# Sinks of two attention forms: their products with V one sub-step later at a chunk's end, and in the second attention in one transpose and one burst for all heads

## The chip, the cores and the metric

The kernel runs on one core of a Trainium2 chip. The metric is the device time of one execution, in microseconds (us). The engines' names in the profile are PE (TensorE, with PEld for its weight loads), DVE (VectorE), ACT (ScalarE), POOL (GpSimd) and SP (SyncE, which issues most DMAs).

## What is computed

Attention with a window of 128 and 4 sink positions, over 4 batches, 8 heads, 768 positions and 64 columns a head; its result, seen as 3072 tokens of 512 columns, goes through a gated product with three weight matrices.

```python
keep = is_sink | in_window              # pos < 4, or 0 <= q - k < 128
scores = np.where(keep, scale * q @ k.T, -1e9)
a = np.exp(scores - scores.max(-1, keepdims=True))
a = a / (a.sum(-1, keepdims=True) + 1e-9)
x = (a @ v).transpose(0, 2, 1, 3).reshape(3072, 512)
out = (x @ w_a) * (x @ w_b) @ w_out     # w_a, w_b: 512 x 1536, w_out: 1536 x 512
```

The reference's inputs give each block of 128 queries (a *tile*) three parts of keys: its own block, the block before it, and the 4 sinks.

## The kernel before

**Stages.** The first tiles of the four batches are done ahead (`first_tiles`). Then come chunks: batch 0's tiles 1 and 2 (the *second attention*, exact float32, `first_attention` with `parts_exact` and `pipeline`), four chunks of three tiles of one batch, and two chunks of three tiles from two batches (two *segments*); these six go through `attention` with `parts_split`, where each float32 operand is a high and a low part. While chunk c's gated product (`moe`) runs on TensorE, the attention of chunk c+1 is woven in: `moe` calls `between(s)` at 33 places, and that takes the attention's generator forward by some of its sub-steps (a `yield` each), 21 of the second attention's and 30 of the others'. What is left then is taken after `moe`. A scheduler sets the final order of each engine's instructions, except where they are kept in program order. It follows priorities by program order and moves an instruction where it thinks that its inputs are late.

**The gated product.** For each of 12 blocks of columns, `moe` makes a (12 products of 128 columns of weights, L846: four blocks kk of x, three high/low combinations each), copies it to g on ScalarE (L883), makes b (L846), multiplies on VectorE (L889), splits the result into gh on ScalarE (L892) and gl (L894) on GpSimd, in the chunk of the first tiles on VectorE, and projects the block before (L873, named o_0, o_1, ... by tile). At a chunk's end the outputs are copied (L904) and written (L905); x of the next chunk is split by ScalarE's cast xh (L829) and VectorE's subtraction xl (L830), block by block. x lies in four parts xf[0] to xf[3], one for each pair of heads.

**Sinks, attention().** The scores (L628) give p for the window and for 4 sinks; a predicated copy (L633) and a reduction (L634) read them from the one PSUM buffer "s". The sinks' columns of all 8 heads lie in one tile sc for each query tile. `sinks_t` turns them with three transposes (L668), and ScalarE, VectorE and ScalarE split them (L670 to L672). `sinks_av(m)` multiplies those of pair m with V of the sinks (L679), and VectorE adds the product to xf[m] (L681). Pairs 0 and 2 take PSUM bank "t", 1 and 3 bank "av"; `av` of a pair (L659) uses "av" too and is copied to xf by ScalarE (L661). V of the sinks comes in two groups (pairs 0, 1 and pairs 2, 3), loaded by `prep_sinks` (L435) and split by GpSimd in `split_sinks` (round, L387, and rest, L390). With two segments both groups lie in one region, since each group then holds one part for each segment.

**Sinks, second attention.** p of a pair of heads gives a sc of 8 columns. `sinks_t(pr)` turns it (L777, 8 rows of 128 columns), VectorE copies it into ptx (L779), and `sinks_av(pr)` multiplies it with the pair's V of the sinks (L784, K of 8) and adds to xf (L786). Transposes (L757), `av` (L769) and sinks share one PSUM bank "t" in two halves; one tile stands for the whole bank.

## Time and profile before

| | |
|---|---|
| Median of 3 runs | 757.16 us (756.3 to 757.17) |
| Profiled execution | 756.8 us, span 755.1 us |
| TensorE busy | 745.2 us, 99 % of the span |
| VectorE, ScalarE, GpSimd busy | 389.8, 387.4, 275.5 us |
| Granted TensorE clock | 0.999 of full speed |

The span is the stretch that the profiler sees; the execution's time includes a little around it. A row of a timeline gives an instruction's start, its length, engine, line, operation and tiles; matmuls are pipelined, so the record of one (0.40 us for 512 columns) is longer than the distance to the next start, and it is distances of starts that add up. A bracket names idle time of the engine ahead and what ended it.

### The profile page before, as it was taken

Reading aid. Unit: us, or ns where it says so; the run is one execution under the profiler, and the core shown is the slowest. Engines: PE = TensorE matmul, PEld = TensorE weight load, DVE = VectorE, ACT = ScalarE, POOL = GpSimd, SP = SyncE. Lnnn points to the kernel's source line nnn. Section 1 sums busy time; section 2 is a strip of 40 time slices with the busy share of each in tenths; the row PEclk is TensorE's granted clock in tenths of the full one; section 3 lists DMA queues with packets and bytes.
Section 4 is the critical chain, followed back from the end, with each engine's and each line's share of the span. In section 5 each row is a group of like instructions: output and inputs, shape, how many; then the busy total and the mean of one; then the engine's idle time right before and its main releaser. Section 6 shows DMA issues by size and latency. Waiting matters only on the chain.

```text
span 755.1 us, 13078 instructions
## 1 busy us (share of the span) xinstructions
PE 745.2 (99%) x4422; PEld 665.7 (88%) x4422; DVE 389.8 (52%) x1303; ACT 387.4 (51%) x1185; POOL 275.5 (36%) x358
## 2 busy tenths in 40 slices
PE   8999999999999999999999999999999999999996
PEld 6877777889899998999989999899989999999996
DVE  6899998455455553445544554355553555331001
ACT  6777765466455663555535555355554655331111
POOL 2200021176425542355404545056561764201110
PEclk9999999999999999999999999999999999999999
DMA  9997111322213343124422344124443141010001
GB/s 333 394 318 279 33 40 40 118 72 75 64 46 85 105 141 92 57 85 123 132 82 70 96 126 138 63 75 124 115 121 114 47 132 47 2 42 1 1 1 44
DMA packets 48807, 76.89 MB, mean 102 GB/s; under 512 B 5056, under 2 KB 28640, under 8 KB 48736
## 3 DMA queue, kind: packets, MB, share of 16 engines
q1 hardware_dynamic: 45568, 70.50, 29.6%
q10 hardware_dynamic: 3168, 5.51, 1.9%
q8 instruction: 36, 0.59, 0.3%
q14 instruction: 35, 0.29, 0.1%
HBM read 69.70 MB, written 6.29 MB: 101 GB/s over the span
## 4 chain that ended last, share of the span: by engine, by line
PE 90%; DMA 3%; DVE 3%; ACT 1%; POOL 1%; issue 1%; SPq 0%; DVEq 0%; POOLq 0%; ACTq 0%
PE a L846 26%; PE o L873 25%; PE b L846 25%; PE s L628 5%; PE av L659 5%; PE t L648 2%; DMA raw_a<-in_wa_dram 1%; DMA raw_o<-in_wo_dram 1%; DMA v<-in_v_dram 1%; PE sk L679 1%; PE s L732 1%; DMA qr<-in_qT_dram 1%; PE t L757 0%; PE t L769 0%; DVE wf_o L348 0%
## 5 line engine op out<-in xcount | busy, mean ns | idle before, releaser
L846 PE MATMUL a<-xh,w_a 128*128 128x384 f32 (+2 forms) x760 | 212.3, 342 | 0.1
L846 PE MATMUL b<-xh,w_b 128*128 128x384 f32 (+2 forms) x760 | 209.9, 340 | 0.5 <-DVE w_b L366 0.5
L873 PE MATMUL o<-w_o,gh 128*128 128x512 f32 x576 | 182.4, 398 | 0.0
L894 POOL TENSOR_TENSOR gl<-g,gh 128x384 fp32r<-128x384 f32 (+1 forms) x70 | 68.2, 974 | 225.9 <-ACT gh L892 221.6
L846 PEld LDWEIGHTS a<-xh,w_a 128*128 128x128 f32 x760 | 137.2, 188 | 8.3 <-issue 1.7
L846 PEld LDWEIGHTS b<-xh,w_b 128*128 128x128 f32 x760 | 137.2, 188 | 5.8 <-issue 1.0
L846 PE MATMUL a<-xl,w_a 128*128 128x384 f32 (+2 forms) x380 | 127.8, 336 | 0.0
L846 PE MATMUL b<-xl,w_b 128*128 128x384 f32 (+2 forms) x380 | 127.7, 336 | 0.0
L873 PEld LDWEIGHTS o<-w_o,gh 128*128 128x128 f32 x576 | 103.9, 188 | 18.8 <-issue 0.9
L873 PE MATMUL o<-w_o,gl 128*128 128x512 f32 x288 | 113.3, 394 | 0.0
L889 DVE TENSOR_TENSOR g<-b,g 128x384 f32<-128x384 f32 (+2 forms) x95 | 52.8, 555 | 112.6 <-PE b L846 111.5
L636 ACT ACTIVATE p<-p,st 128x132 f32<-128x132 f32 x144 | 58.0, 403 | 74.4 <-DVE st L634 73.2
L892 ACT CAST gh<-g 128x384 fp32r<-128x384 f32 (+2 forms) x96 | 49.3, 513 | 88.6 <-DVE g L889 88.6
L883 ACT COPY g<-a 128x384 f32<-128x384 f32 (+2 forms) x95 | 45.0, 474 | 91.2 <-PE a L846 85.7
L633 DVE COPY_PREDICATED s<-own,s 128x128 f32<-128x128 uint16 x144 | 42.0, 291 | 82.0 <-PE s L628 80.4
L846 PEld LDWEIGHTS a<-xl,w_a 128*128 128x128 f32 x380 | 71.4, 188 | 2.7
L639 ACT ACTIVATE p<-p,st 128x132 f32<-128x132 f32 x144 | 58.2, 404 | 29.3 <-DVE st L638 28.6
L846 PEld LDWEIGHTS b<-xl,w_b 128*128 128x128 f32 x380 | 71.4, 188 | 1.7
L390 POOL TENSOR_TENSOR ks<-kr,ks 64x524 fp32r<-64x524 f32 (+1 forms) x64 | 70.4, 1110 | 3.9
L873 PEld LDWEIGHTS o<-w_o,gl 128*128 128x128 f32 x288 | 54.1, 188 | 12.9 <-DVE gl L894 0.9
L637 DVE TENSOR_SCALAR st<-st 128x1 f32<-128x1 f32 x144 | 21.9, 152 | 74.8 <-ACT p L636 74.8
L387 POOL TENSOR_SCALAR qh<-qr 128x384 fp32r<-128x384 f32 x48 | 24.9, 519 | 86.4 <-DMA qr<-in_qT_dram 49.4
(166 smaller groups left out, 1029.7 us busy)
## 6 DMA issues: line engine op xcount, KB each, us to landing
raw_a<-in_wa_dram SPq DMA_DIRECT2D x12, 512.0 KB, 7.8
raw_b<-in_wb_dram SPq DMA_DIRECT2D x12, 512.0 KB, 6.3
raw_o<-in_wo_dram SPq DMA_DIRECT2D x12, 512.0 KB, 6.9
qr<-in_qT_dram SPq DMA_DIRECT2D x32, 192.0 KB, 2.6
chk_a<-in_wa_dram SPq DMA_DIRECT2D x24, 256.0 KB, 3.2
chk_b<-in_wb_dram SPq DMA_DIRECT2D x24, 256.0 KB, 3.0
chk_o<-in_wo_dram SPq DMA_DIRECT2D x24, 256.0 KB, 3.1
out_dram<-os ACTq DMA_DIRECT2D x21, 256.0 KB, 2.1
```

The costliest lines, as they stand in the source:

```text
L390: self.nc.gpsimd.tensor_tensor(o, i, high.bitcast(F32), op=ALU.subtract)
L628: nc.tensor.matmul(ps, lhsT=q[:, i * P:(i + 1) * P], rhs=ks[:, c0s[i]:c0s[i] + SW], start=n == 0, stop=n == 1)
L633: nc.vector.copy_predicated(ps[:, :P], self.own.bitcast(mybir.dt.uint16), ps[:, W:])
L636: nc.scalar.activation(p, p, AF.Exp, bias=st[:, 0:1], scale=-1.0, accum_out=st[:, 1:2])
L639: nc.scalar.mul(p, p, st[:, 3:4])
L659: nc.tensor.matmul(ps[half[e], c * P:(c + ns) * P], lhsT=v[:, e, blk, :], rhs=pt[:, e, sl:sl + ns, :], start=j == 0, stop=j == len(groups) ...
L846: mm = self.nc.tensor.matmul(ps[:, cols], lhsT=w[:, ksl], rhs=x[:, kk, cols], start=start and kk == 0 and i == 0, stop=kk == NK - 1 and i ...
L873: nc.tensor.matmul(outs[i], lhsT=g[:, sl], rhs=w, start=j == 0 and k == 0, stop=j == NJ - 1 and k == 2)
L883: nc.scalar.copy(g[:, :n], pa[:, :n])
L889: nc.vector.tensor_tensor(g[:, :n], pb[:, :n], g[:, :n], op=ALU.mult)
L892: nc.scalar.copy(gh[:, :n], g[:, :n])
L894: e.tensor_tensor(gl[:, :n], g[:, :n], gh[:, :n].bitcast(F32), op=ALU.subtract)
```

## The change

In `attention`, `sinks_av(0)`, `sinks_av(1)` and `split(1)` move from the last sub-step of h = 8 to the first one of h = 9; `sinks_av(2)` and `(3)` stay in the second and third. In `parts_exact` and `pipeline` the sinks of all heads are collected in one tile of 32 columns and turned by one transpose, the turned sinks lie in a buffer of the tag "p" (sks) instead of in ptx, the loads of V of the sinks are two instead of four, with all 32 rows and zeros for the other heads' rows (the array vS holds them so), and the four products with K of 32 follow in two sub-steps at the end. The parameter `group` goes. Lines behind the change have lower numbers after it (L846 is L840 after, L873 is L867, L679 is L677).

```diff
--- before.py
+++ after.py
@@ -558,7 +558,7 @@
         (_, t0, nt), = segs
         late = [i for i in range(nt) if t0 + i >= 2]
         units = [(h, i) for h in range(H) for i in range(nt)]
-        return self.pipeline(units, nt, late, *self.parts_exact(*segs[0], xf, after), 2, 2, 1)
+        return self.pipeline(units, nt, late, *self.parts_exact(*segs[0], xf, after), 2, 1)
 
     def attention(self, parts, xf, after):
 
@@ -583,15 +583,13 @@
                         split(0)
                 if i == 1 and 1 <= h <= H:
                     transposes(h - 1)
-                if h == H:
-                    if i == 1:
-                        sinks_t()
-                    elif i == 2:
-                        sinks_av(0, xf)
+                if h == H and i == 1:
+                    sinks_t()
+                elif h > H:
+                    sinks_av(i + (i > 0), xf)
+                    if i == 0:
                         sinks_av(1, xf)
                         split(1)
-                elif h > H and i:
-                    sinks_av(i + 1, xf)
                 yield
 
     def parts_split(self, segs):
@@ -714,11 +712,11 @@
                 nc.sync.dma_start(v[:, :, :nb], self.vB[b, h // 2, :, :, s0:s0 + nb])
             else:
                 v = preps[h - 1][2]
-                if late:
-                    vs = ptx[:2 * NS, h // 2 % 2, 2 * nt + 1, :]
-                    m = h // 2
-                    nc.sync.dma_start(vs, self.vS[b, m * 2 * NS:(m + 1) * 2 * NS, m])
-                    vss[h // 2] = vs
+                if late and h < 4:
+                    vs = ptx[:H * NS, h // 2, 2 * nt:2 * nt + 2, :]
+                    nc.sync.dma_start(vs, self.vS[b, :H * NS, h - 1:h + 1])
+                    for c in range(2):
+                        vss[h - 1 + c] = vs[:, c, :]
             preps[h] = k, q, v
 
         def scores(h, i):
@@ -742,9 +740,9 @@
             nc.scalar.mul(p[:, :w], p[:, :w], st[:, 3:4])
             state[h, i] = p
             if i in late:
-                if h % 2 == 0:
-                    sc[h // 2, i] = self.at.tile([P, 2, NS], F32, tag=f"sc{i % 3}", name=f"sc{u}", bufs=2)
-                nc.gpsimd.tensor_copy(sc[h // 2, i][:, h % 2, :], p[:, P:P + NS])
+                if h == 0:
+                    sc[i] = self.at.tile([P, H, NS], F32, tag=f"sc{i}", name=f"sc{u}", bufs=2)
+                nc.gpsimd.tensor_copy(sc[i][:, h, :], p[:, P:P + NS])
 
         def transposes(h, i):
             p = state.pop((h, i))
@@ -770,30 +768,31 @@
                                          start=m == 0, stop=m == len(blks) - 1)
             nc.scalar.copy(xf[h // 2][:, :nt * P].rearrange("p (c q) -> p c q", q=P), ps[:, :nt, :])
 
-        def sinks_t(pr):
+        def sinks_t():
             n = len(late)
-            tp = half_bank(0, f"skt{tag}_{pr}")
+            tp = half_bank(0, f"skt{tag}")
             for k, i in enumerate(late):
-                nc.tensor.transpose(tp[:2 * NS, k, :], sc[pr, i].rearrange("p a b -> p (a b)"), self.ident)
-            skt[pr] = ptx[:2 * NS, pr % 2, 2 * nt:2 * nt + n, :]
-            nc.vector.tensor_copy(skt[pr], tp[:2 * NS, :n, :])
-
-        def sinks_av(pr, _):
+                nc.tensor.transpose(tp[:H * NS, k, :], sc[i].rearrange("p a b -> p (a b)"), self.ident)
+            s = self.at.tile([P, SW], F32, tag="p", name=f"sks{tag}")
+            skt[0] = s[:H * NS, :n * P].rearrange("p (k q) -> p k q", q=P)
+            nc.vector.tensor_copy(skt[0], tp[:H * NS, :n, :])
+
+        def sinks_av(pr):
             n = len(late)
             ps = half_bank(1, f"sk{tag}_{pr}")
-            nc.tensor.matmul(ps[:, :n, :], lhsT=vss[pr], rhs=skt.pop(pr), start=True, stop=True)
+            nc.tensor.matmul(ps[:, :n, :], lhsT=vss[pr], rhs=skt[0], start=True, stop=True)
             xs = xf[pr][:, late[0] * P:nt * P].rearrange("p (c q) -> p c q", q=P)
             nc.vector.tensor_tensor(xs, ps[:, :n, :], xs, op=ALU.add)
 
         return do_prep, scores, transposes, av, sinks_t, sinks_av
 
-    def pipeline(self, units, nt, late, do_prep, scores, transposes, av, sinks_t, sinks_av, lag, group, early):
+    def pipeline(self, units, nt, late, do_prep, scores, transposes, av, sinks_t, sinks_av, lag, early):
 
         for h in range(early):
             do_prep(h)
         yield
         nu = len(units)
-        for k in range(nu + lag + 2 + group // 2):
+        for k in range(nu + lag + 3):
             if k < nu:
                 h, i = units[k]
                 if i == 0:
@@ -801,21 +800,16 @@
                 scores(h, i)
             n = k - lag - 1
             if 0 <= n < nu and units[n][1] == nt - 1:
-                h = units[n][0]
-                av(h)
-                if h % group == group - 1 and late:
-                    sinks_t(h // group)
-            for c in range(group // 2):
-                n -= 1
-                if 0 <= n < nu and units[n][1] == nt - 1:
-                    h = units[n][0]
-                    if h % group == group - 1 and late:
-                        sinks_av(h // group, c)
-            n = k - lag
-            if 0 <= n < nu:
-                transposes(*units[n])
+                av(units[n][0])
+            if k == nu + lag - 1 and late:
+                transposes(*units[-1])
+                sinks_t()
+            elif 0 <= k - lag < nu:
+                transposes(*units[k - lag])
+            if k > nu + lag and late:
+                for c in range(2):
+                    sinks_av(2 * (k - nu - lag - 1) + c)
             yield
-
 
     def new_x(self, nt):
         n = max(nt, 3) * P
```

**The last project of the chunk, on TensorE.** Names are bank or tile, then pair, head or block: o_3 is the first tiles' fourth output, a_0 and b_0 are the next chunk's first products, s_3_0_0 its first scores; t_1_0_0_628 is the shared bank. Before:

```order
L873 MATMUL o_3_485<-w_o_1588,gh_11_1620 128x512 x2
L873 MATMUL o_3_485<-w_o_1588,gl_11_1621 128x512
L846 MATMUL a_0_1680<-xh,w_a_385 128x256
L846 MATMUL a_0_1680<-xl,w_a_385 128x256
L846 MATMUL a_0_1680<-xh,w_a_385 128x256 x2
L846 MATMUL a_0_1680<-xl,w_a_385 128x256
L846 MATMUL a_0_1680<-xh,w_a_385 128x256 x2
L846 MATMUL a_0_1680<-xl,w_a_385 128x256
L846 MATMUL a_0_1680<-xh,w_a_385 128x256 x2
L846 MATMUL a_0_1680<-xl,w_a_385 128x256
L846 MATMUL a_0_1680<-xh,w_a_385 128x256
L628 MATMUL s_3_0_0_1695<-ks_3_0_1322,qh_3_0_1323 128x260
```

The twelve a products, then the scores, follow the project at once. After (L783 is a sinks' product):

```order
L867 MATMUL o_3_485<-w_o_1574,gh_11_1606 128x512 x2
L867 MATMUL o_3_485<-w_o_1574,gl_11_1607 128x512
L783 MATMUL t_1_0_0_628<-sks_1_1479,ptx 128x128
L840 MATMUL a_0_1670<-xh,w_a_385 128x256
L840 MATMUL a_0_1670<-xl,w_a_385 128x256
L840 MATMUL a_0_1670<-xh,w_a_385 128x256 x2
L783 MATMUL t_1_0_0_628<-sks_1_1479,ptx 128x128
L840 MATMUL a_0_1670<-xl,w_a_385 128x256
L840 MATMUL a_0_1670<-xh,w_a_385 128x256
L626 MATMUL s_3_0_0_1685<-ks_3_0_1309,qh_3_0_1310 128x260
L626 MATMUL s_3_0_0_1685<-ks_3_0_1309,ql_3_0_1311 128x260
L840 MATMUL b_0_1709<-xh,w_b_419 128x256
```

Two of the four sinks' products stand behind the project, and a_0's first two blocks come first; the other two blocks of a_0 and b_0 stand in the rows that follow, behind the scores:

```order
L626 MATMUL s_3_0_1_1727<-ks_3_0_1309,qh_3_0_1310 128x260
L626 MATMUL s_3_0_1_1727<-ks_3_0_1309,ql_3_0_1311 128x260
L840 MATMUL a_0_1670<-xh,w_a_385 128x256
L840 MATMUL b_0_1709<-xh,w_b_419 128x256
L840 MATMUL a_0_1670<-xl,w_a_385 128x256
L840 MATMUL a_0_1670<-xh,w_a_385 128x256
L840 MATMUL b_0_1709<-xl,w_b_419 128x256
L840 MATMUL b_0_1709<-xh,w_b_419 128x256
L626 MATMUL s_3_0_2_1740<-ks_3_0_1309,qh_3_0_1310 128x260
L626 MATMUL s_3_0_2_1740<-ks_3_0_1309,ql_3_0_1311 128x260
L840 MATMUL a_0_1670<-xh,w_a_385 128x256
```

The same products stood in one row of twelve before.

**The end of a two-segment chunk, on TensorE.** sk_4_0 to sk_4_3 are the sinks' products of the pairs, av_4_3 the attention product of pair 3. Before:

```order
L846 MATMUL b_9_6849<-xh,w_b_1380 128x384
L679 MATMUL sk_4_0_6867<-xh,xl 128x256
L679 MATMUL sk_4_0_6867<-xh,xl 128x128
L679 MATMUL sk_4_1_6871<-xh,xl 128x256
L679 MATMUL sk_4_1_6871<-xh,xl 128x128
L873 MATMUL o_0_5892<-w_o_1421,gh_8_6789 128x512 x2
L873 MATMUL o_0_5892<-w_o_1421,gl_8_6790 128x512
L873 MATMUL o_1_5893<-w_o_1421,gh_8_6789 128x512 x2
```

Behind two more outputs come av_4_3 and all of a_10, and then sk_4_2. After:

```order
L657 MATMUL av_4_3_6866<-pt,v_4_3_6590 64x256 x2
L657 MATMUL av_4_3_6866<-pt,v_4_3_6590 64x128 x8
L677 MATMUL sk_4_0_6878<-xh,xl 128x256
L677 MATMUL sk_4_0_6878<-xh,xl 128x128
L840 MATMUL a_10_6894<-xh,w_a_1427 128x384
L840 MATMUL a_10_6894<-xl,w_a_1427 128x384
L677 MATMUL sk_4_1_6882<-xh,xl 128x256
L677 MATMUL sk_4_1_6882<-xh,xl 128x128
L840 MATMUL a_10_6894<-xh,w_a_1427 128x384 x2
L840 MATMUL a_10_6894<-xl,w_a_1427 128x384
L840 MATMUL a_10_6894<-xh,w_a_1427 128x384 x2
L840 MATMUL a_10_6894<-xl,w_a_1427 128x384
```

sk_4_0 and sk_4_1 moved behind the project and av_4_3; ten products of a_10 stand between sk_4_1 and sk_4_2, where the whole project, av_4_3 and a_10 stood.

**The same place on GpSimd.** vsr is the loaded V of the sinks, which GpSimd splits into the region xl. Before:

```order
L387 TENSOR_SCALAR qh_4_1_7061<-qr_4_1_7057 128x384
L390 TENSOR_TENSOR ql_4_1_7062<-qr_4_1_7057,qh_4_1_7061 128x384
L387 TENSOR_SCALAR xl<-vsr_4_1_1_6715 128x256
L387 TENSOR_SCALAR xl<-vsr_4_1_2_6717 128x256
L390 TENSOR_TENSOR xl<-vsr_4_1_1_6715,xl 64x256
L390 TENSOR_TENSOR xl<-vsr_4_1_2_6717,xl 64x256
L894 TENSOR_TENSOR gl_9_6864<-g_9_6835,gh_9_6863 128x384
```

The split stands ahead of the low part gl_9. After, on GpSimd:

```order
L387 TENSOR_SCALAR qh_4_1_7051<-qr_4_1_7047 128x384
L390 TENSOR_TENSOR ql_4_1_7052<-qr_4_1_7047,qh_4_1_7051 128x384
L888 TENSOR_TENSOR gl_9_6854<-g_9_6825,gh_9_6853 128x384
L387 TENSOR_SCALAR xl<-vsr_4_1_1_6705 128x256
L387 TENSOR_SCALAR xl<-vsr_4_1_2_6707 128x256
L390 TENSOR_TENSOR xl<-vsr_4_1_1_6705,xl 64x256
L390 TENSOR_TENSOR xl<-vsr_4_1_2_6707,xl 64x256
```

The low part gl_9 now runs ahead of the split.

## Rows read from the trace of the kernel before

**Rows 1.** The page: busy time (share) and instructions; the chain's shares by engine.

```profile
PE 745.2 (99%) x4422; PEld 665.7 (88%) x4422; DVE 389.8 (52%) x1303; ACT 387.4 (51%) x1185; POOL 275.5 (36%) x358
...
PE 90%; DMA 3%; DVE 3%; ACT 1%; POOL 1%; issue 1%; SPq 0%; DVEq 0%; POOLq 0%; ACTq 0%
```

**Rows 2.** Timeline, second attention (start, us, engine, line, operation, [idle before <-releaser]).

```profile
106.49 0.40 PE L846 MATMUL a<-xl,w_a 128*128 128x512 f32 x1
...
107.51 0.44 PE L757 MATMUL t<-ident,p 128*128 128x128 f32 x2 [0.62 <-DVE ptx L779]
...
113.07 1.81 POOL L390 TENSOR_TENSOR ks<-kr,ks 64x524 fp32r<-64x524 f32 x1
...
113.96 1.47 DVE L894 TENSOR_TENSOR gl<-g,gh 128x512 fp32r<-128x512 f32 x1
...
114.63 0.40 PE L873 MATMUL o<-w_o,gh 128*128 128x512 f32 x1
...
115.36 0.28 DVE L786 TENSOR_TENSOR xf<-t,xf 128x128 f32<-128x128 f32 x1
...
115.69 0.44 PE L757 MATMUL t<-ident,p 128*128 128x128 f32 x2 [0.66 <-DVE st L740]
...
142.79 0.69 DVE L894 TENSOR_TENSOR gl<-g,gh 128x512 fp32r<-128x512 f32 x1 [0.69 <-ACT gh L892]
```

**Rows 3.** Timeline of PE at a small transpose of the second attention.

```profile
62.57 0.40 PE L846 MATMUL a<-xh,w_a 128*128 128x512 f32 x1
...
62.80 0.28 PE L777 MATMUL t<-ident,sc 128*8 128x128 f32 x1
...
63.15 0.39 PE L846 MATMUL a<-xl,w_a 128*128 128x512 f32 x1
```

**Rows 4.** Timelines at the end of the second attention's chunk, by engine.

```profile
139.23 0.41 ACT L829 CAST xh<-xf 128x256 fp32r<-128x256 f32 x1
...
139.67 0.43 DVE L830 TENSOR_TENSOR xl<-xf,xh 128x256 fp32r<-128x256 f32 x1 [3.73 <-ACT xh L829]
...
146.50 0.39 PE L873 MATMUL o<-w_o,gl 128*128 128x512 f32 x1
146.73 0.28 PE L846 MATMUL a<-xh,w_a 128*128 128x256 f32 x1
...
148.23 0.28 PE L628 MATMUL s<-ks,ql 128*128 128x260 f32 x1
...
148.88 0.29 DVE L634 CUSTOM_DVE_ANT_0 p<-s,mg 128x132 f32<-128x132 f32 x1
```

**Rows 5.** Timelines of PE at the end of the first two attention() chunks.

```profile
200.82 0.63 PE L873 MATMUL o<-w_o,gh 128*128 128x512 f32 x2
...
201.41 0.62 PE L679 MATMUL sk<-xh,xl 128*128 128x384 f32 x2
...
286.81 0.34 PE L846 MATMUL b<-xh,w_b 128*128 128x384 f32 x1
...
287.34 0.61 PE L679 MATMUL sk<-xh,xl 128*128 128x384 f32 x2 [0.19 <-ACT xh L672]
...
287.79 0.39 PE L873 MATMUL o<-w_o,gh 128*128 128x512 f32 x1
```

**Rows 6.** Timelines at the end of a two-segment chunk: PE, POOL and ACT.

```profile
654.23 0.57 PE L679 MATMUL sk<-xh,xl 128*128 128x256 f32 x4
...
654.83 0.78 POOL L387 TENSOR_SCALAR xl<-vsr 128x256 fp32r<-128x256 f32 x2 [5.33 <-PE sk L679]
...
655.69 1.44 POOL L390 TENSOR_TENSOR xl<-vsr,xl 64x256 fp32r<-64x256 f32 x2
...
658.31 0.44 PE L846 MATMUL a<-xh,w_a 128*128 128x384 f32 x1
...
658.43 0.48 ACT L661 COPY xf<-av 128x384 f32<-128x384 f32 x1 [2.82 <-PE av L659]
...
660.49 0.34 PE L679 MATMUL sk<-xh,xl 128*128 128x256 f32 x2
```

## The prediction

> **What bounds the kernel now.** First the page. TensorE is busy for 745.2 of the span's 755.1 us, the other engines for 36 to 52 %, and the chain that ended last runs through TensorE for 90 % [rows 1]. So the change matters only where it makes TensorE issue more or fewer instructions, or removes or makes a wait of TensorE. Next I read TensorE's waits by what they waited for, and then timelines round each place: the second attention, the joint between its chunk and the next, and the end of an attention() chunk, with one segment and with two. TensorE is back to back nearly everywhere there, and the distance of two starts is then the price of the first instruction: 0.23 us for 512 columns (146.50 to 146.73) [rows 4], 0.12 for 256 (146.73 to 148.23 is 1.50 for thirteen steps), and 0.18 for 384 (658.31 to 660.49 is 2.18 for twelve) [rows 6]. A distance above that is time lost. In the part that is changed three rows carry a wait of their own: 0.62 and 0.66 us in the second attention, for VectorE [rows 2], and 0.19 us at the end of an attention() chunk, for ScalarE [rows 5].
>
> **The change, part by part** (against the profiled execution, 756.8 us; the median is 0.36 above it).
>
> *Second attention, waits for the bank.* All its small work shares one PSUM bank. The transposes of a block wait until VectorE has read it: once the copy of a small transpose, once the addition of the sinks' product. A product starts at 106.49, the transposes should follow 0.23 later, and start at 107.51: 0.79 lost. From 114.63 to 115.69 it is 0.83 [rows 2]. That second row names a statistic (L740) as what it waited for; on VectorE the addition L786 at 115.36 stands just ahead of that, behind a subtraction of 1.47 us, and I take the addition to be the cause, since the transposes need the bank that it reads. In the new order both VectorE instructions are gone from in front of these transposes; what is left to wait for is ScalarE's copy of the block before, which I count as done by then. Gain 0.79 + 0.83 = **1.62**.
>
> *Three small transposes fewer.* Two products with a small transpose between take 0.58 (62.57 to 63.15) [rows 3], the two alone 0.46: 0.12 each, **0.36** gained. Four sinks products stand against four, with 128 columns each and 32 rows instead of 8. No row shows one with 32; I take no difference, and as bound on either side one such break each, 4 × 0.12 = 0.5. The three VectorE copies and two DMA issues that go, and the 32-row copy and wider loads that come, lie beside other work: the copy has a project and the following a and b products to land in before the first product needs it.
>
> *Joint of second attention and next chunk.* The last two of these products fall behind the chunk's last project. Before, TensorE passes there without a gap (146.50, 146.73) [rows 4]. After, the new chunk's first a product can do two of its four blocks, and the others wait for product, addition, ScalarE's cast and VectorE's subtraction; scores and b products are put in between. One buffer holds the scores, so the second tile's scores wait for predicated copy and reduction of the first: 0.94 from the start of the last score product (148.23) to the reduction's end (148.88 + 0.29), with 0.82 of work in seven steps between, so 0.2 lost with a hand-over. The low half of block 2 is subtracted only behind the second tile's predicated copy: 0.65 from the score product to there (148.23 to 148.88) + 0.43 (139.67) + 0.05 = 1.1, with 0.36 of work in three steps between: 0.7 lost. The buffer costs 0.2 to 0.4 again at the next head's first tile; some of that kind may stand in the stretch of before, and I leave 0.2. Together **+1.1**; bounds 0.3 (the subtractions come ahead of the scores' copies, only the hand-overs stay) and 2.5 (the series below, mostly uncovered).
>
> *End of attention() chunks.* The products of pairs 0 and 1 move behind a project and pair 3's attention product, some 4 us later (654.23 against 658.31) [rows 6]. In the second such chunk TensorE reached them too early: 286.81 to 287.34 is 0.53 where 0.18 is usual, 0.35 lost. In the first, two 512-column products at 200.82 should give way at 201.28 and the sinks come at 201.41: 0.13 lost. Restarting costs 0.1 more each (two 384-column products should take 0.36, and 287.34 to 287.79 is 0.45) [rows 5]. Together **0.68** gained; in the other four chunks nothing is waited for there. Pair 1's product now also needs ScalarE's copy of pair 3's result, whose bank it takes: the copy ends 0.60 behind the next product's start (658.31; 658.43 + 0.48), and pair 0's sinks and two products, three times 0.18 and something for the start, stand in between [rows 6]. Hidden, or nearly.
>
> *Two-segment chunks, GpSimd.* Both groups of split sinks lie in one region, so GpSimd can split the second only when pair 1's product has read the first. Before, it waits 5.33 us for that, starts 0.03 after the product's end (654.23 + 0.57), and its four instructions end at 655.69 + 1.44 = 657.13: 2.30 in all, while the first product that needs them stands at 660.49 [rows 6]; 3.4 us of slack. After, pair 1 stands behind pair 0's sinks and two a products (each 384 columns, 0.18), so it starts about 0.6 behind A = 658.31 and is over some 0.4 later, at A + 1.0. The split is done at A + 3.3. TensorE has the twelve a products (2.18) and two pairs of sinks (0.36) to run and stands at pair 2 at A + 2.54. It waits 0.8, in two chunks: **+1.6**. Bounds: 0, if the split's parts are taken up as they come (the first segment's is ready at 1.0 + 0.86 + 0.72 = A + 2.6) and the rest is covered; 1.3 each, if pair 1 waits 0.4 for ScalarE's copy and a restart is paid. GpSimd's low part of the gated product now runs ahead of the split instead of behind; it is needed a whole b product later, so no one waits for it.
>
> Sum: −1.62 − 0.36 + 1.1 − 0.68 + 1.6 = +0.04: 756.84 in the profiled execution, **757.2** as a median, no change. About 0.2 %, 1.5 us, is what a measurement of this kernel can tell from none.
>
> **Rivals.**
> *Faster: the new chains are covered.* The joint at its lower end and no wait for the split: −2.66 + 0.3 = −2.36, 754.4, median 754.8. For it: the planner put ten a products between pairs 1 and 2, and all the filling it had into the joint. Against: GpSimd's times are read directly, and its start can't be earlier than the product's end. It decides if both places together cost less than 1.2.
> *Slower: the joint runs in series.* Two additions (0.28), two casts (0.41), two subtractions (0.43) come to 2.24 [rows 2, 4]; with one tile's predicated copy (0.65 with its scores) between on VectorE 2.9. If TensorE's filling stands behind these waits in its own order and so covers none, the joint costs 2.9 instead of 1.1: 758.6, median 759.0. For it: TensorE takes its instructions in the order written, and so do ScalarE, which still copies the last outputs there, and VectorE. Against: some 2 us of scores and b products lie ahead of the waits. It decides when the joint costs more than 2.6.
> *Slower: the bank waits move.* Both 0.8 were lost because VectorE was late with other work: the subtraction took 1.47 at 113.96, beside GpSimd's 1.81 us at 113.07, and 0.69 at 142.79, with no such neighbour [rows 2]. If another instruction of that stretch then is what TensorE waits for, the 1.62 do not come: 758.46, median 758.8. For it: VectorE is the fullest engine but TensorE [rows 1], and none of GpSimd's work goes. Against: TensorE needs the subtraction only with the next project. The Trainium skill (page "SBUF — State Buffer", section "Who interferes with whom") says that VectorE and GpSimd take a shared port in turns when a VectorE instruction reads two operands from SBUF. By that rule the subtraction stays at 1.47 after the change, and the sum is this rival's if TensorE comes to wait for it; the trace agrees as far as 1.47 against 0.69 shows it.
> That the change doesn't do what it says is ruled out by the order, but for one thing: only half of the "one burst" falls inside the chunk, and the joint above prices that.
>
> **How the numbers follow.** No change 0.58; faster, by the first rival, 0.20; slower, by the second 0.14 and the third 0.08. So faster by over 0.2 % 0.20, within it 0.58, slower 0.22. The range leaves out 0.2: from 755.0, where the first rival begins to be left out (0.13 below), to 759.0, at the second's price (0.07 above).
>
> **What would show it.** TensorE's two waits for VectorE in the second attention gone, with the transposes 0.23 behind the product: step one. No wait for the turned sinks at the end of the first two attention() chunks: step four. TensorE waiting 0.8 us for GpSimd ahead of pair 2's sinks in both two-segment chunks: step five; if it doesn't, the slack was under-read. At the joint, waits for reduction and subtraction of about 1.1 together: step three. The forecast is wrong if VectorE's lateness in the second attention turns up in front of another product, or if the sinks' additions at a chunk's end hold up the gated product on VectorE and with it the project.

## The result and the profile after

| | before | after |
|---|---|---|
| Median | 757.1 us (756.3 to 757.71, 6 runs) | 761.35 us (760.77 to 762.91, 6 runs) |
| Profiled execution, span | 756.8, 755.1 | 760.84, 759.1 |
| TensorE busy | 745.2 | 746.9 |

The ratio is 1.0059 (95 % interval 1.0049 to 1.0069): slower by 0.5 to 0.7 %, outside the range. The page of after, its first part (compare [rows 1]):

```profile
PE 746.9 (98%) x4419; PEld 666.9 (88%) x4419; DVE 390.9 (51%) x1300; ACT 386.6 (51%) x1185; POOL 278.1 (37%) x358
```

No engine has notably more to do: of the span's 4.0 us TensorE is busy for 1.7 and idle for 2.3 (a busy record is longer than the work, so waits in part show as busy). TensorE's waits in after, by what they waited for (us in total, times, longest):

```profile
PE t L767 <- DVE sks L778: 1.7, 1, 1.7
...
PE s L626 <- DVE st L632: 1.2, 1, 1.2
PE sk L677 <- POOL xl L390: 0.6, 2, 0.3
PE a L840 <- DVE xl L824: 0.5, 1, 0.5
```

The two bank waits of [rows 2] and the wait on the turned sinks of [rows 5] are gone; four others have come. Two of these the prediction had priced (GpSimd's split, the joint's subtraction), two it had not: 1.7 us for the copy of the turned sinks, 1.2 us for a score buffer.

Where the time went is read best by counting: both traces hold 3144 matmuls of the gated product (a, b, o) in nearly the same order, so I subtract the start of the n-th in before from that in after, from the first on (30.82 and 31.20 us; most of the 0.38 ahead of it is a DMA that TensorE waits for early on and that landed later, at 7.78 instead of 7.49, which differs from profile to profile by as much). The growth by stretch; the last column has the prediction's terms, and for each sinks product that changes its place 0.55 to 0.6, an estimate of mine, since the prediction set four products against four and priced none:

| stretch (time in before) | growth, us | predicted |
|---|---|---|
| second attention to 119.4 | −3.99 | −3.6 (1.62, three small transposes at 0.12, and three sinks products that move behind it, some 0.55 each) |
| to 126.3: project 8, pair 3's attention product, in after the turn | +2.22 | about 0.1 |
| to 135.5: two sinks products for one, a small transpose less | +0.52 | +0.5 |
| to 153.0: the joint | +2.28 | 1.1 and two sinks products, 1.2 |
| to 167.9: the second head of the next chunk | +1.39 | 0 |
| ends of the one-segment chunks | −0.24, −0.44 | −0.68 |
| ends of the two-segment chunks | +0.70, +0.78 | +1.6 |

These come to +3.22; small drifts elsewhere bring it to +3.51 at the last product. With the 0.38 at the start this is the span's 4.0 less 0.1. Two stretches, 2.22 and 1.39, hold the whole miss.

**The first.** Timeline of after round pair 3's attention product (start, length, engine, line, tiles):

```profile
118.92 0.38 PE L755 MATMUL t<-ident,p 128*128 128x128 f32 x2
...
119.86 0.27 PE L775 MATMUL t<-ident,sc 128*32 128x128 f32 x1
...
122.40 0.68 DVE L883 TENSOR_TENSOR g<-b,g 128x512 f32<-128x512 f32 x1
123.00 0.68 DVE L348 CUSTOM_DVE_ANT_0 wf_b<-raw_b,wf_b 128x1024 uint16<-128x1024 uint16 x1
123.60 0.27 DVE L778 COPY sks<-t 32x128 f32<-32x128 f32 x1
...
123.93 1.09 PE L767 MATMUL t<-ptx,vx 128*64 128x128 f32 x16 [1.72 <-DVE sks L778]
```

The sinks are turned at 119.86 into the shared bank. VectorE copies them only at 123.60: it works without a gap, and the copy stands in its order behind weight work, the gated product g and one more weight step. Pair 3's attention product needs the same bank and stands ahead of any sinks product. By the count it starts 1.8 later for it; 0.14 of the stretch is the turn, and 0.3 a wait for VectorE's w_b some 7 us before.

Under this lies VectorE's own pace. It was as full in before as in after, and its work hardly came earlier: the gated product g, at 122.40 in after, stood at 122.87 in before, 0.85 earlier when the start's 0.38 is taken off, while TensorE's products there were 3.6 to 4.0 earlier. Most of TensorE's gain to 119.4 was thus a lead on VectorE, and shrank where TensorE next needed VectorE, first at the weights, then at the copy. Weight load of TensorE in after, g in before, then 120 to 124 us of before and of after (busy time and counts of TensorE, its weight loads, VectorE, ScalarE and GpSimd, then the clock as a share of 2.4 GHz, DMA share, GB/s):

```profile
116.48 0.30 PEld L840 LDWEIGHTS b<-xh,w_b 128*128 128x128 f32 x2 [0.46 <-DVE w_b L366]
...
122.87 0.68 DVE L889 TENSOR_TENSOR g<-b,g 128x512 f32<-128x512 f32 x1
...
120.00:124.00 4.00, 4.00 (x20) 3.25 (x19) 3.83 (x7) 2.64 (x6) 0.00 (x0) 1.00 0.00 0
...
120.00:124.00 4.00, 2.28 (x13) 1.55 (x13) 3.84 (x8) 1.12 (x3) 0.00 (x0) 1.00 0.00 0
```

This is read from the rows. No run here made VectorE earlier at this place, so whether the lead would then have been kept is not shown.

**The second.** Timeline of after, from GpSimd to TensorE (gl, g, exp, statistic, predicated copy, scores):

```profile
153.35 1.31 POOL L390 TENSOR_TENSOR ks<-kr,ks 64x524 fp32r<-64x524 f32 x1
154.75 0.74 POOL L888 TENSOR_TENSOR gl<-g,gh 128x256 fp32r<-128x256 f32 x1
...
155.51 0.37 ACT L877 COPY g<-a 128x256 f32<-128x256 f32 x1 [1.70 <-PE s L626]
...
155.88 0.41 ACT L634 ACTIVATE p<-p,st 128x132 f32<-128x132 f32 x1
...
156.41 0.15 DVE L635 TENSOR_SCALAR st<-st 128x1 f32<-128x1 f32 x1 [1.87 <-ACT p L634]
...
157.02 0.28 DVE L631 COPY_PREDICATED s<-own,s 128x128 f32<-128x128 uint16 x1
...
158.52 0.36 PE L626 MATMUL s<-ks,qh 128*128 128x260 f32 x1 [1.20 <-DVE st L632]
```

In before, GpSimd's low part of the chunk's first gated product ran at 151.03, ahead of four splits for the next head:

```profile
151.03 0.73 POOL L894 TENSOR_TENSOR gl<-g,gh 128x256 fp32r<-128x256 f32 x1 [8.45 <-ACT gh L892]
```

In after it stands behind them, at 154.75. There is one buffer g: ScalarE's copy of the next a waits until GpSimd has read it (154.75 + 0.74 = 155.49, start 155.51). The row names TensorE as releaser, which had long been done. The exp queues behind that copy, VectorE's next predicated copy behind the exp's statistic, and TensorE's scores behind the one score buffer.

**The split.** Timelines of after at the second two-segment chunk (compare [rows 6]): GpSimd starts with the end of pair 1's product and is done at 664.27; TensorE's second half of pair 2 starts at 664.33.

```profile
661.55 0.41 PE L677 MATMUL sk<-xh,xl 128*128 128x256 f32 x2
...
662.00 0.77 POOL L387 TENSOR_SCALAR xl<-vsr 128x256 fp32r<-128x256 f32 x2 [2.28 <-PE sk L677]
662.85 1.42 POOL L390 TENSOR_TENSOR xl<-vsr,xl 64x256 fp32r<-64x256 f32 x2
...
663.64 0.38 PE L677 MATMUL sk<-xh,xl 128*128 128x256 f32 x1
664.33 0.33 PE L677 MATMUL sk<-xh,xl 128*128 128x128 f32 x1 [0.30 <-POOL xl L390]
```

### The profile page after: what moved, and what is told of

It is laid out like the page before. It is cut to its first block, busy times and chain, and to the rows that moved or that the text cites. A ratio compares the mean times of both kernels' runs of the same rounds, so it can differ in the third digit from the quotient of the medians.

```text
span 759.1 us, 13050 instructions
## 1 busy us (share of the span) xinstructions
PE 746.9 (98%) x4419; PEld 666.9 (88%) x4419; DVE 390.9 (51%) x1300; ACT 386.6 (51%) x1185; POOL 278.1 (37%) x358
## 4 chain that ended last, share of the span: by engine, by line
PE 87%; DVE 6%; DMA 3%; issue 1%; POOL 1%; ACT 1%; SPq 0%; DVEq 0%
PE a L840 25%; PE b L840 24%; PE o L867 24%; PE s L626 5%; PE av L657 5%; PE t L646 2%; DMA raw_a<-in_wa_dram 1%; DMA raw_o<-in_wo_dram 1%; DMA v<-in_v_dram 1%; PE sk L677 1%; DVE wf_b L348 1%; PE s L730 0%; DVE w_a L366 0%; DVE wf_a L337 0%; DVE w_o L366 0%
## 5 line engine op out<-in xcount | busy, mean ns | idle before, releaser
L840 PE MATMUL a<-xh,w_a 128*128 128x384 f32 (+2 forms) x760 | 213.2, 342 | 0.1
L840 PE MATMUL b<-xh,w_b 128*128 128x384 f32 (+2 forms) x760 | 210.2, 340 | 0.5 <-DVE w_b L366 0.4
L867 PE MATMUL o<-w_o,gh 128*128 128x512 f32 x576 | 182.2, 398 | 0.0
L840 PEld LDWEIGHTS a<-xh,w_a 128*128 128x128 f32 x760 | 137.5, 188 | 7.1 <-ACT p L634 1.0
L840 PEld LDWEIGHTS b<-xh,w_b 128*128 128x128 f32 x760 | 137.4, 188 | 6.0 <-DVE w_b L366 1.3
L840 PE MATMUL a<-xl,w_a 128*128 128x384 f32 (+2 forms) x380 | 128.0, 337 | 0.5 <-DVE xl L824 0.5
L840 PE MATMUL b<-xl,w_b 128*128 128x384 f32 (+2 forms) x380 | 127.9, 337 | 0.0
L867 PEld LDWEIGHTS o<-w_o,gh 128*128 128x128 f32 x576 | 103.9, 188 | 18.8 <-issue 1.0
L867 PE MATMUL o<-w_o,gl 128*128 128x512 f32 x288 | 113.3, 394 | 0.0
L840 PEld LDWEIGHTS a<-xl,w_a 128*128 128x128 f32 x380 | 71.4, 188 | 3.4 <-DVE xl L824 0.7
L840 PEld LDWEIGHTS b<-xl,w_b 128*128 128x128 f32 x380 | 71.4, 188 | 1.7
L867 PEld LDWEIGHTS o<-w_o,gl 128*128 128x128 f32 x288 | 54.1, 188 | 12.9 <-DVE gl L888 0.9
```

What stands on the lines that cost most here:

```text
L840: mm = self.nc.tensor.matmul(ps[:, cols], lhsT=w[:, ksl], rhs=x[:, kk, cols], start=start and kk == 0 and i == 0, stop=kk == NK - 1 and i ...
L867: nc.tensor.matmul(outs[i], lhsT=g[:, sl], rhs=w, start=j == 0 and k == 0, stop=j == NJ - 1 and k == 2)
```

## Experiments

The theory after the comparison: four places, each with a price of its own, that add up: the copy's wait (1.7 to 2), the joint (1.1), GpSimd's queue behind the joint (1.2 to 1.4), the split (1.5), against 2.3 + 0.7 gained. Growths below are counted like those of the table; medians stand beside those of the kernel before on the same chip.

**One part alone.** `e1` takes the new `attention`, `e2` the new `parts_exact` and `pipeline`.

> Only the move in attention(); the second attention as before. Read from the trace of the changed kernel: the one-segment chunks gain 0.24 + 0.36 (first two), each two-segment chunk loses 0.7 to 0.8 to the wait for GpSimd's split. Theory (the two parts add, each paid where its wait stands): +0.9 us against before, so about 758.0. Rival (the loss of the changed kernel comes from this part, by the sinks' additions that now meet the gated product on VectorE): +3 us or more, 760.

> Only the second attention's part; attention() as before. Theory: it carries the larger loss, from three waits: pair 3's attention product behind VectorE's copy of the turned sinks (1.7 us), the joint (about 1.4 more than the two sinks products that move there), and a wait for the score buffer 10 us later (1.2), against 1.6 + 0.4 gained: +2.5 to +3.3 us, 759.6 to 760.4. Rival (the parts only lose together): within 1 us of before.

Measured: 758.0 against 756.81, ratio 1.0011 (1.0002 to 1.002), and 759.64 against 756.81, 1.0033 (1.0021 to 1.0046). Both theories' numbers hold, the rivals' don't: by the ratios the parts cost about 0.8 and 2.5 us, and most of the loss is the second attention's. The trace of `e2` has the copy's wait (1.7), the score buffer's (1.2) and the subtraction's (0.5).

**The GpSimd chain.** One buffer for the second chunk's first g, nothing else moves:

```diff
-            g = self.mo.tile([P, max(n, 3 * P)], F32, tag="g", ...)
+            own = n == 2 * P and j == 0
+            g = self.mo.tile([P, n if own else max(n, 3 * P)], F32, tag="g_own" if own else "g", ...)
```

> The changed kernel, every engine's order the same, but the first gated product of the chunk behind the joint has a buffer g of its own, so the second one's copy on ScalarE need not wait until GpSimd has read the first. Theory (GpSimd's low part of it is queued 2.5 us later than before, behind four splits for the next head; ScalarE's copy waits for that, the next exp behind the copy, VectorE behind the exp, and TensorE 1.2 us for the score buffer): the 1.2 us wait goes, -1.2 against the changed kernel, about 760.1. Rival (the score buffer is late because VectorE's subtractions of the joint pushed its work back): the wait stays, 761.3.

Measured: 759.77 against 756.81, 1.0038 (1.0023 to 1.0053). The 1.2 us wait is gone from TensorE's list, with GpSimd's low part as late as in after (155.15), and the growth at 167.9 is 1.18 instead of 2.41: −1.23. The chain is shown: it is the single buffer, read late, and not VectorE's subtractions.

**The split.** The two-segment chunks keep the old place:

```diff
+                late_sinks = len(rows) == 1
                 if h == H and i == 1:
                     sinks_t()
-                elif h > H:
-                    sinks_av(i + (i > 0), xf)
-                    if i == 0:
-                        sinks_av(1, xf)
-                        split(1)
+                elif (h, i) == ((H + 1, 0) if late_sinks else (H, 2)):
+                    sinks_av(0, xf)
+                    sinks_av(1, xf)
+                    split(1)
+                elif h > H and i:
+                    sinks_av(i + 1, xf)
...
```

> The changed kernel, but the chunks with two segments keep the old place of pairs 0 and 1 and of the split. Theory (GpSimd's split is on the path there: 0.7 + 0.8 in the two chunks): -1.5 against the changed kernel, +2.7 against before, 759.5, and no wait of TensorE for GpSimd at the sinks. Rival (those chunks lose by something else, the later additions on VectorE): the stretches there stay 0.7 and 0.8 longer than before.

Measured: 758.86 against 756.89, 1.0029 (1.0017 to 1.0041). TensorE's wait for GpSimd is gone, and the end of the trace grows by 1.86 instead of 3.51: −1.65.

The same edit in the kernel before:

> The kernel before, with the move of attention()'s sinks in the one-segment chunks alone. Theory (the terms add): the first two of these chunks gain 0.24 + 0.44, nothing else moves: -0.6 to -0.7 against before, about 756.2. Rival (in some one-segment chunk the later additions hold something up): no gain.

Measured: 756.4 against 756.73, 0.9997 (0.9988 to 1.0005). The trace stands at −0.3 to −0.55 between the chunk ends of mid-kernel and at −0.1 at the last product: what the first two ends gave drifts away again, 0.28 of it at 562.9, where nothing was changed. A gain of 0.6 is within the interval, and so is none.

**The copy, first try: turn behind the attention product.**

```diff
-            if k == nu + lag - 1 and late:
-                transposes(*units[-1])
+            if k == nu + lag and late:
                 sinks_t()
-            elif 0 <= k - lag < nu:
+            if 0 <= k - lag < nu:
```

> The changed kernel, but the sinks are turned behind pair 3's attention product, not ahead of it, so nothing of that bank stands between the turn and the first sinks product. Theory (that product waited 1.7 us because the turned sinks stood in its bank and VectorE's copy of them came late): TensorE's wait for the copy goes or falls under 0.3, -1.5 us against the changed kernel, about 759.8. Rival (VectorE is late with whatever stands there, the wait only moves to the first sinks product): no gain, 761.3, and a wait of 1 us or more ahead of the first sinks product.

Measured: 760.0 against 756.81, 1.004 (1.0025 to 1.0055). By the medians this looks like a gain on 761.35, and the theory's 759.8; by the count it is none (2.33 at 167.9 against 2.41), and the intervals of the two ratios overlap. The attention product waits no more, but the turn now waits for ScalarE, and the second sinks product for VectorE's addition, as TensorE's rows in the timeline of `e3` show:

```profile
122.49 1.09 PE L767 MATMUL t<-ptx,vx 128*64 128x128 f32 x16
...
125.20 0.27 PE L775 MATMUL t<-ident,sc 128*32 128x128 f32 x1 [0.73 <-ACT xf L769]
...
132.55 0.48 PE L783 MATMUL t<-sks,ptx 32*128 32x128 f32 x2 [0.63 <-DVE xf L785]
```

The rival was right in that the wait moved, in two pieces, though to the turn and the second sinks product and not to the first.

**All four products inside the chunk.** 22 sub-steps instead of 21 (`steps = ... H * len(nrows) + 6`).

> The changed kernel with one sub-step more of the second attention taken inside its chunk (22 instead of 21), so that all four sinks products stand ahead of the last project and GpSimd's order at the joint is that of before. Read from the trace of the changed kernel, the stretch from the project ahead of the joint to the second project behind it grew by 2.25 + 1.31, of which some 1.0 is the two products themselves, which only move. Theory (the joint and GpSimd's queue there cost 2.5): -2.5 against the changed kernel, +1.8 against before, about 758.6. Rival (VectorE is late in this chunk whatever its place, so the same waits come earlier, in front of the four products): less than 1 us gained, above 760.

Measured: 759.84 against 756.89, 1.0041 (1.0028 to 1.0055). Both were half right. The joint is free: growth 1.84 at 143.9, 1.86 at 167.9, and neither wait of the joint is left. But the sub-steps come earlier, and to 135.5 the kernel has lost 1.85 where after had gained 1.25: the copy's wait is 1.9, and the products and their additions stand closer. Of these 3.1 us the clock has a part: behind the wait it was granted at 0.59 for 4 us in this profile, which by an estimate (4 × 0.41) is 1.6 us. The window of `e4`, columns as above:

```profile
122.00:126.00 4.00, 4.00 (x19) 3.09 (x16) 3.95 (x10) 2.77 (x6) 0.00 (x0) 0.59 0.23 66
```

**The copy on ScalarE, in that kernel**, and with the split's place mended as well:

```diff
-            nc.vector.tensor_copy(skt[0], tp[:H * NS, :n, :])
+            nc.scalar.copy(skt[0], tp[:H * NS, :n, :])
```

> The kernel with all sinks inside (22 sub-steps), and the copy of the turned sinks is ScalarE's instead of VectorE's; there it stands right behind the copy of the last block. Theory (the copy came late since it stands behind some 3 us of weight work on VectorE, and pair 3's attention product waits for the bank): the 1.7 us wait goes, -1.5 against that kernel, 757.0 to 757.4. Rival (what stands behind it moves to ScalarE's own lateness, or the wait comes back ahead of the first sinks product): within 0.5 of it.

> All inside, the copy on ScalarE, and the move in attention() for the one-segment chunks alone. If the terms add: 1.6 + 0.4 gained from the second attention's bank waits and small transposes, 0.6 from the one-segment chunks, nothing lost at the joint, for the copy or for GpSimd: -2.6 against before, about 754.4. Rival (at most the bank waits' gain is left, or the copy's wait stays): 755.5 to 757.

Measured: 763.19 and 761.88 against 756.89, 1.0082 (1.0061 to 1.0102) and 1.0069 (1.0045 to 1.0093): the first is the slowest of all. The copy's wait went, and the second sinks product, which now came early, waited 3.2 us for VectorE's addition of the first. The clock fell behind that wait (windows in the last section: 4 × 0.46 + 4 × 0.50, some 3.8 us), so more of the loss is the clock's than the wait's. Timelines of `e8`, TensorE and VectorE:

```profile
126.40 0.48 PE L783 MATMUL t<-sks,ptx 32*128 32x128 f32 x2
...
129.46 1.26 DVE L348 CUSTOM_DVE_ANT_0 wf_o<-raw_o,wf_o 128x1024 uint16<-128x1024 uint16 x1
130.64 0.28 DVE L785 TENSOR_TENSOR xf<-t,xf 128x128 f32<-128x128 f32 x1
...
130.98 0.48 PE L783 MATMUL t<-sks,ptx 32*128 32x128 f32 x2 [3.20 <-DVE xf L785]
```

**VectorE's load.** Low parts of the first tiles' gated products on GpSimd: 6 to 8 in the changed kernel, 5 to 7 in the kernel before (with the one-segment move), 5 to 8 with all sinks inside (with that move too).

```diff
-            e = nc.gpsimd if weights_split and j < NJ - 2 else nc.vector
+            e = nc.gpsimd if (j < NJ - 2 if weights_split else j in (6, 7, 8)) else nc.vector
```

> The changed kernel, but in the chunk of the first tiles the low parts of the gated products 6, 7 and 8 are GpSimd's and not VectorE's (2.0 us less in VectorE's queue ahead of the copy of the turned sinks; GpSimd had 4 us without work at 112 to 116 us and 12 us behind). Theory (VectorE runs some 3 us behind TensorE there, and the copy stands at the end of that queue): the 1.7 us wait of pair 3's attention product falls to 0.5 or less, -1.2 or more against the changed kernel, about 759.8. Rival (the copy is late since it stands behind the gated product 9, which follows TensorE's own b product): the wait stays above 1.4.

> The kernel before with the move in the one-segment chunks alone, and the low parts of the first tiles' gated products 5, 6 and 7 on GpSimd. Theory (the two bank waits of before, 0.8 each, come from VectorE's lateness alone): they shrink below 0.3 each without touching the sinks, -0.65 - 1.0 or more against before, about 755.3. Rival (GpSimd's low parts come late or lock VectorE out): no gain or a loss, a wait of TensorE for GpSimd ahead of a project.

> The kernel with all sinks inside their chunk, the move in the one-segment chunks alone, and the low parts 5 to 8 on GpSimd. Theory (the burst loses by VectorE's lateness only): the waits for the copy and between the four products fall from about 5 to 2, 756.5 to 757.5. Rival (the burst is a chain of VectorE turns through one bank, late or not): still 758.5 or more.

Measured: 762.04, 757.3 and 760.96 against 756.73; ratios 1.0072 (1.0059 to 1.0085), 1.0008 (0.9999 to 1.0016), 1.0063 (1.005 to 1.0076). No gain; in `e11` one bank wait of before shrank to 0.2 us, the other grew to 0.9, and one of 0.4 for ScalarE came. In `e10` the copy's wait is 1.72 as in after, which is the rival's number, but not by its ground: g ran back to back with VectorE's work, and waited for no b product. VectorE loses most of what it gives away (2.0 us): two steps beside GpSimd's low parts took 1.1 and 0.5 us longer than in after. This goes by the rule that the prediction cites from the Trainium skill (page "SBUF — State Buffer", section "Who interferes with whom"), that the two take a shared port in turns; the trace agrees as far as these rows show it: GpSimd's low part took 1.29 us at 115.96, and VectorE's w_b beside it 1.18, where the same step took 0.67 at 115.76 in after. Timelines of `e10`, VectorE and TensorE:

```profile
116.63 1.18 DVE L366 TENSOR_TENSOR w_b<-wf_b,w_b 128x512 fp32r<-128x512 f32 x1
...
124.98 0.27 DVE L778 COPY sks<-t 32x128 f32<-32x128 f32 x1
...
125.31 1.09 PE L767 MATMUL t<-ptx,vx 128*64 128x128 f32 x16 [1.72 <-DVE sks L778]
```

From w_b to the copy VectorE's rows are back to back in both kernels, 115.76 to 123.60 and 116.63 to 124.98: the copy is as late as the instructions ahead of it in the order are long.

**The copy out of VectorE's order, products in place.** The changed kernel with the copy on ScalarE, and the turn taken one `between` earlier (`+ (c == 0 and s == 3 * 9)` on the sub-steps wanted); then the same with the buffer of `e5` and the place of `e6`.

> The changed kernel, but the turn of the sinks is taken one place earlier (ahead of the b product 9 instead of behind it) and its copy is ScalarE's; pair 3's attention product and the four sinks products keep their places. Theory (the copy's place in VectorE's order, behind some 8 us of weight work and the gated product 9, is what makes it late; ScalarE has time right behind its last block's copy): the 1.7 us wait goes and nothing else moves, -1.5 to -1.9 against the changed kernel, about 759.5. Rival (pair 3's product or the first sinks product then waits for VectorE elsewhere, as it did with the turn behind the product and with all sinks inside): less than 0.5 gained.

> As the kernel with the copy on ScalarE one place earlier, and also a buffer g of its own for the first gated product behind the joint, and the move in attention() in the one-segment chunks alone. If the four terms add (3.5 lost in the changed kernel, 1.7 for the copy, 1.2 for g, 1.7 for GpSimd's split): -1.1 against before, about 755.7, faster than both. Rival (the terms overlap): as before, 756.8, or slower.

Measured: 760.64 against 756.99, 1.0051 (1.0037 to 1.0064), and 758.24 against 756.99, 1.0014 (1.0005 to 1.0023). The copy ran at 118.97, and pair 3's product started without a wait. So the place in VectorE's order made it late. But of the 1.7 only 0.1 came back (2.31 at 167.9 against 2.41), as the rival had it: in the earlier sub-step the last block's transposes and the turn each wait for ScalarE. Three orders, after, `e3` and `e13`, lose TensorE's lead at different waits, for VectorE or for ScalarE, and stand at −1.25, −1.35 and −1.35 at 135.5. So the copy's wait is where the loss shows in after; taking that wait away did not bring it back. Timelines of `e13`, TensorE and ScalarE:

```profile
116.75 0.44 PE L755 MATMUL t<-ident,p 128*128 128x128 f32 x2 [0.77 <-ACT ptx L756]
...
118.67 0.27 PE L775 MATMUL t<-ident,sc 128*32 128x128 f32 x1 [0.56 <-ACT ptx L756]
...
118.97 0.26 ACT L778 COPY sks<-t 32x128 f32<-32x128 f32 x1 [0.45 <-PE t L775]
...
123.53 1.09 PE L767 MATMUL t<-ptx,vx 128*64 128x128 f32 x16
```

`e14` adds the two mended terms (1.23 + 1.65): 3.51 − 0.1 − 2.88 is 0.5, and its ratio's interval is 0.4 to 1.7 us. Its expectation, faster than both kernels, missed. Its trace, of its slowest execution (759.85), stands not at 0.5 but at 2.57: TensorE waits 0.95 us for VectorE's addition, ahead of the second sinks product, which it does not in `e13`, and behind that the clock was low, some 1.7 us by an estimate (4 × 0.42). The window of `e14`:

```profile
134.00:138.00 4.00, 4.00 (x12) 3.12 (x11) 2.48 (x5) 0.70 (x2) 0.00 (x0) 0.58 0.61 197
```

So that the terms add is borne out by the median and not by that trace; by the sum, what is left of the loss is the copy's stretch and the joint. No kernel here is faster than before by more than the measurement tells; `e9` is the nearest. A second bank for the second attention's small work was not tried: the kernel's eight PSUM tags are all in use there.

## Why the prediction was wrong

- *Waits for the bank, small transposes, −1.62 and −0.36*: they came. The rows with waits of [rows 2] have no counterpart in after, and the stretch to 119.4 gave −3.99 against −3.6. They were not kept: by the rows of the first stretch most of the gain was a lead on VectorE.
- *The 32-row copy at nothing*: this step failed. The prediction named as cover "a project and the following a and b products", up to the first product that needs the copied sinks. The first to wait is another: pair 3's attention product, which needs not the sinks but the bank they lie in. The prediction had read that very pattern in before (transposes that wait until VectorE has read the bank) and did not ask the question again for the new instruction. In VectorE's order some 8 us of work stand between the last tile's statistic and the copy (115.76 to 123.60). The wait is 1.7 of the stretch's 2.22. What the runs leave open is how much of it any order could have saved: with the copy out of VectorE's order 0.1 came back. The prediction's own sign of being wrong, that VectorE's lateness turns up in front of another product, is what came.
- *GpSimd at the joint*: not in the prediction at all. Its text weighed GpSimd's order at the two-segment chunks and not at the joint, where the low part of the chunk's first gated product fell behind four splits; the copy to the single g made that a wait of 1.2 us, five steps further on. The step that failed is the list of queues that the joint's moved instructions pass.
- *The joint, +1.1*: right, 2.28 with the two products of 1.2.
- *One-segment ends −0.68, split +1.6*: right, −0.68 and +1.48. In the second chunk pair 2's second half starts 0.57 late (663.64 to 664.33, where 0.12 is usual), against 0.8; the rest of that chunk's 0.78 is not taken apart. At the one-segment ends the gain stands, but in `e9` −0.1 of it is left at the end.
- *The rivals.* The third had the mechanism, the bank waits move to another place of a VectorE that is late, though its 758.8 left out GpSimd's queue at the joint; but its ground, the subtraction stretched by GpSimd, was not it. In after the low part took 0.68 at 114.44, and the stretched one was another, a weight step: 1.68 at 111.29, beside GpSimd's 1.37 us at 111.05. The sentence that by the rule the subtraction stays at 1.47 was wrong in that: by the same rule of the Trainium skill two that meet lock each other out, and which two meet the new order decides.
- *The sum*: with 2.22 and 1.39 in their places the forecast of 757.2 becomes 760.8, against the median of 761.35.

## What to carry to other kernels

When several small operations share one PSUM bank, gathering them into one burst makes each turn of the bank wait for the same queue, one after the other; spread out, each has the distance to the next as cover. For every new reader of a buffer ask who writes that buffer next, not only who needs the result. And of a moved step, follow every engine's order at the new place to the first instruction with a single buffer: the price may stand five steps away. And when TensorE gains beside an engine that has no time to spare, ask whether that engine comes earlier too; if not, the gain may be a lead that the next wait takes back.

## Unexpected of the hardware

After a wait of TensorE the granted clock sometimes falls to the lower level, 1.2 GHz, and the length of the wait doesn't tell alone. Windows of `e8`, columns as above: the first holds part of the wait of 3.2 us, and TensorE did 1.02 us of work in it; the clock is at half speed behind it:

```profile
128.00:132.00 4.00, 1.02 (x5) 0.82 (x6) 3.25 (x7) 0.00 (x0) 1.98 (x2) 1.00 0.43 116
132.00:136.00 4.00, 4.00 (x11) 2.68 (x10) 1.33 (x3) 0.35 (x1) 0.00 (x0) 0.54 0.22 56
136.00:140.00 4.00, 4.00 (x10) 2.65 (x9) 1.69 (x4) 1.31 (x3) 0.00 (x0) 0.50 0.00 0
```

Of 1.7 us, the copy's wait was followed by 1.00 in the profile of after, and by 0.69 in that of `e2`, which has the same wait at the same place; `e2` lost 1.5 us more there:

```profile
122.00:126.00 4.00, 2.28 (x22) 1.73 (x22) 4.00 (x9) 2.14 (x5) 0.00 (x0) 1.00 0.00 0
...
126.00:130.00 4.00, 4.00 (x19) 3.23 (x18) 3.77 (x8) 1.63 (x3) 1.08 (x2) 1.00 0.60 186
```

```profile
126.00:130.00 4.00, 4.00 (x14) 3.15 (x13) 3.76 (x7) 0.94 (x3) 1.45 (x2) 0.69 0.61 186
```

The first fence is after's, the second `e2`'s. Of after's six executions three have a mean granted clock of 0.995 to 0.996 and times of 761.85 to 762.91, the others 0.998 to 1.0 and 760.77 to 760.84. In the profile of `e12` TensorE waited for 1.24, 1.40 and 1.43 us between 118 and 134 us, and the clock stayed at 1.00. So a wait seems to have a second price that is paid in some executions, here some 1 to 2 us, and that goes with the spread of the times of after; where the clock fell in its three longer executions was not traced.
